# An MLP's first product over pairs of token blocks: seven block products for eight, and channel mix and MLP in two loops

## The chip, the cores and the metric

The kernel runs on one core of a Trainium2 chip. The metric is the device time of one execution in microseconds; the kernel before has a median of 2599.82 us over three runs (2597.92 to 2599.9).

## What is computed

Squared-relu attention over 4 sequences of 3072 tokens, an RWKV channel mix, and a squared-relu MLP, all in float32. Inputs are u, v (4 x 3072 x 256), z (4 x 3072 x 64), and weights.

```python
def _attn_ref(u, v, z):
    scale = 1.0 / S
    scores = scale * np.matmul(z, z.transpose(0, 2, 1))
    attn = np.maximum(scores, 0.0) ** 2
    return u * np.matmul(attn, v)

def _moe_ref(x, mu_k, mu_r, w_k, w_v, w_r):      # w_k 256 x 1024, w_v 1024 x 256, w_r 256 x 256
    xk = mu_k * x + (1.0 - mu_k) * x_prev        # x_prev: the token before
    xr = mu_r * x + (1.0 - mu_r) * x_prev
    k = np.maximum(xk @ w_k, 0.0)
    v = k * k @ w_v
    return 1.0 / (1.0 + np.exp(-(xr @ w_r))) * v

def _moe2_ref(x, w_in, w_out):                   # w_in 256 x 2048, w_out 2048 x 256
    r = np.maximum(x @ w_in, 0.0)
    return r * r @ w_out
```

## The kernel before

The work is done on transposed tiles: 128 features on partitions, a block of T = 512 tokens along the free dimension; there are NBLK = 24 blocks. Every float32 product is made of three matmuls on values split into a high and a low part (`split`, lines 80 to 85): high x high, low weight x high, high weight x low. One matmul is 128 x 128 weights against 128 x 512 values.

Attention comes first (`attention`, line 232): scores, squared relu, and the product with v, with the weights' conversion from float64 between. Its result goes to memory as `xT`, block by block. The first block of the channel mix (`up1`, `down1`) is already worked into its end.

Then `channel_mix_and_mlp` (line 499) runs over the 24 blocks, and within a block over 16 hidden tiles f of the MLP. At each f it makes the hidden tile f + 1 (`up2`: 6 matmuls at line 203, then relu and square on ScalarE, lines 157 and 158, cast and low part on VectorE, lines 84 and 85) and adds hidden tile f into the two output accumulators (`down2`: 6 matmuls, lines 534, 535 and 538). Between these, by the tables `before`, `after` and `aside` (lines 583 to 595), stand the pieces of the channel mix for the next block: `up1` and `down1` for its 8 hidden tiles, `gate_r`, `gate_v`, and `mix`. `gate_v` (line 515) multiplies the accumulators by the sigmoid and splits the product into the MLP's input, which stays on the chip. The schedule is manual: each engine runs its instructions in the order in which the program writes them.

The MLP's weights lie in memory as float32; `load_piece` and `split_piece` bring them in, the first two before the loop, the rest during block 0. A block's result is scaled out of the accumulators (line 560), transposed (line 561) and stored by four DMAs (`store`). For the last block the down products run in two halves of 256 tokens (`down2_half`, line 550), so that the first half's store overlaps the second's matmuls.

PSUM has eight banks: in this loop two for the channel mix's accumulators (`ps_v`), four for the MLP's (`ps_o`), two for hidden products (`ps_u`).

Of the kernel before, what the change touches and what calls it, by code (L numbers as in the profile page):

```python
# [7 lines left out]
F32 = mybir.dt.float32  # L8
# [8 lines left out]
Q = 32  # L17
# [4 lines left out]
def tile_relu2_attention__rwkv_channel_mix__relu2_mlp(  # L22
# [41 lines left out]
    perm = ctx.enter_context(tc.tile_pool(name="perm", bufs=1))  # L64
    raw_p = ctx.enter_context(tc.tile_pool(name="raw", bufs=3))
    ps_v = ctx.enter_context(tc.tile_pool(name="ps_v", bufs=1, space=PSUM))
    el = ctx.enter_context(tc.tile_pool(name="el", bufs=4))
# [6 lines left out]
    w_out32 = dram.tile([F2, D], F32, name="w_out32")  # L74
    xT = [dram.tile([D, S], F32, name=f"xT{b}") for b in range(B)]
# [136 lines left out]
    def down1(n, f):  # L212
        if f == 0:
            acc_v[n] = acc_tiles()
# [10 lines left out]
    AHEAD = 2  # L225

# [5 lines left out]
    def attention():  # L232
        with ExitStack() as st:
# [3 lines left out]
            ps_a = st.enter_context(tc.tile_pool(name="ps_a", bufs=1, space=PSUM))  # L237
            ps_w = st.enter_context(tc.tile_pool(name="ps_s", bufs=4, space=PSUM))
# [227 lines left out]
            for i in range(AHEAD):  # L466
                at_step(s + 12, load_piece, i)
# [31 lines left out]
    def channel_mix_and_mlp():  # L499
        with ExitStack() as st:  # L500
            wp = st.enter_context(tc.tile_pool(name="wp", bufs=1, reuse_waits="tile"))
            ps_o = st.enter_context(tc.tile_pool(name="ps_o", bufs=2, space=PSUM, reuse_waits="tile"))
            ps_w = st.enter_context(tc.tile_pool(name="ps_u", bufs=2, space=PSUM, reuse_waits="tile"))
            win = [wp.tile([P, 2, ND, T], F32R, name=f"win{i}") for i in range(F2 // T)]
            wout = [wp.tile([P, 2, G, D], F32R, name=f"wout{i}") for i in range(NF2 // G)]
            pools["ps"], pools["hidden"] = ps_w, (wp, "h", 6)
            gt, acc_o, x2, sig = {}, {}, {}, {}

            def gate_r(n, d):
                ps = up(lambda h, c, f: wr[:, h, c, f * P:(f + 1) * P], xr_t[n], d)  # L510
                t = wp.tile([P, T], F32, tag=f"sig{d}", name="sig")
                nc.scalar.activation(out=t, in_=ps, func=AF.Sigmoid)
                sig[n, d] = t

            def gate_v(n, d):
                if d == 0:
                    x2[n] = wp.tile([P, 2, ND, T], F32R, tag="x2", name="x2", bufs=2)
                t = el.tile([P, T], F32, tag="a", name="x2f")
                nc.vector.tensor_tensor(out=t, in0=acc_v[n][d], in1=sig.pop((n, d)), op=ALU.mult)
                split(x2[n][:, 0, d, :], x2[n][:, 1, d, :], t)  # L520

            def up2(n, f):
                q, r = divmod(f, T // P)
                ps = up(lambda h, c, f: win[q][:, h, c, r * P:(r + 1) * P], x2[n], f)
                gt[n, f] = relu2_split(ps, HS)

            def down2(n, f):
                if f == 0:
                    acc_o[n] = [ps_o.tile([P, T], F32, tag=f"o{d}", name=f"o{d}") for d in range(ND)]
                hi, lo = gt.pop((n, f))  # L530
                w, c = wout[f // G], f % G
                for d in range(ND):
                    ds_ = slice(d * P, (d + 1) * P)
                    nc.tensor.matmul(acc_o[n][d], lhsT=w[:, 0, c, ds_], rhs=hi, start=f == 0, stop=False)  # L534
                    nc.tensor.matmul(acc_o[n][d], lhsT=w[:, 1, c, ds_], rhs=hi, start=False, stop=False)  # L535
                for d in range(ND):
                    ds_ = slice(d * P, (d + 1) * P)
                    nc.tensor.matmul(acc_o[n][d], lhsT=w[:, 0, c, ds_], rhs=lo, start=False, stop=f == NF2 - 1)  # L538

            def down2_half(n, f, half):  # L540

                if f == 0:
                    acc_o[n, half] = ([ps_o.tile([P, T], F32, tag=f"o{d}", name=f"o{d}") for d in range(ND)] if half == 0
                                      else acc_tiles())
                (hi, lo), w, c = gt[n, f], wout[f // G], f % G
                ts = slice(half * T // 2, (half + 1) * T // 2)
                for d in range(ND):
                    ds_ = slice(d * P, (d + 1) * P)
                    for k, (h, x) in enumerate(((0, hi), (1, hi), (0, lo))):
                        nc.tensor.matmul(acc_o[n, half][d][:, 0:T // 2], lhsT=w[:, h, c, ds_], rhs=x[:, ts],  # L550
                                         start=f == 0 and k == 0, stop=f == NF2 - 1 and k == 2)

            def store(n, half=None, engines=(nc.sync,) * (P // Q)):

                y = raw_p.tile([P, T // Q, ND, Q], F32, tag="raw", name="y")
                a, size = acc_o.pop(n if half is None else (n, half)), T if half is None else T // 2
                m, t0 = size // Q, n * T + (half or 0) * size
                for d in range(ND):
                    t = wp.tile([P, T], F32, tag="yT", name="yT", bufs=2)
                    nc.scalar.mul(t[:, 0:size], a[d][:, 0:size], HS**-2)  # L560
                    nc.vector.transpose(y[:, 0:m, d, :], t[:, 0:size].rearrange("x (k q) -> x k q", q=Q))
                w = ND * Q
                for p, e in enumerate(engines):
                    e.dma_start(out=out[t0:t0 + size, p * w:(p + 1) * w].rearrange("(k q) f -> q k f", q=Q),
                                in_=y[p * Q:(p + 1) * Q, 0:m].rearrange("q k d r -> q k (d r)"))

            def split_piece(i):
                _, cs, fs = w_pieces[i]
                if i % 2 == 0:
                    t = win[fs.start // T]  # L570
                    split_raw(("w32", i), t[:, 0, cs], t[:, 1, cs])
                else:
                    t = wout[cs.start // G]

                    src = raws.pop(("w32", i)).rearrange("x c (p d r) -> x c p d r", d=ND, r=Q)
                    for d in range(ND):
                        split(*(t[:, h, :, d * P:(d + 1) * P].rearrange("x c (p r) -> x c p r", r=Q) for h in range(2)),
                              src[:, :, :, d], True)
                load_piece(i + AHEAD)

            before, after, aside = {}, {}, {}
            for f, unit, a in ((0, up1, 2), (1, down1, 1), (2, up1, 3), (3, down1, 2), (4, up1, 4), (5, down1, 3),
                               (6, up1, 5), (7, down1, 4), (8, up1, 6), (9, down1, 5), (10, gate_r, 0),
                               (11, gate_r, 1), (12, down1, 7)):
                before[f] = (1, unit, a)
            after[9] = (1, up1, 7)
            after[10] = (1, down1, 6)
            before[13], before[14] = (2, up1, 0), (2, up1, 1)  # L590
            before[15] = (2, down1, 0)
            aside[1], aside[2] = (1, mix, 1, 0), (1, mix, 1, 1)
            aside[3] = (2, load_x)
            aside[7], aside[9] = (2, mix, 0, 0), (2, mix, 0, 1)
            aside[12], aside[13] = (1, gate_v, 0), (1, gate_v, 1)
            assert NF1 == 8 and NF2 == 16

            def run(n, what):
                if what and n + what[0] < NBLK:
                    what[1](n + what[0], *what[2:])  # L600

            gate_r(0, 0)
            gate_v(0, 0)
            split_piece(0)
            gate_r(0, 1)
            gate_v(0, 1)
            split_piece(1)
            for f in range(3):
                up1(1, f)
            up2(0, 0)  # L610


            last, TAIL = NBLK - 1, 4
            for n in range(NBLK):
                for f in range(NF2):
                    if n < last:
# [5 lines left out]
                        if n == 0 and f % 4 < 2 and f // 4 < 3:  # L622
                            split_piece(2 + f // 4 * 2 + f % 4)
# [45 lines left out]
```

## Time and profile before

| | |
|---|---|
| runs | 2597.92, 2599.82, 2599.9 us; median 2599.82 |
| the profiled execution: its span, first to last instruction | 2597.3 us |
| what lies around that span | not recorded by itself; the three runs are 0.6 to 2.6 us above it |
| mean granted TensorE clock | 0.999 |
| from 0 to about 980 us | attention, with block 0 of the channel mix at its end |
| from about 980 to 2592 us | the channel mix of 23 blocks and the MLP of 24, interleaved |
| mean share of the DMA engines after 1000 us | 0.06 to 0.09 |

Matmuls are pipelined: a matmul's own duration overlaps that of the next, so the spacing of starts is the price of one. Idle time of an engine counts only where the engine that sets the end waits for it.

### The profile page before, as it was taken

How to read it: one execution, taken by the hardware profiler on the slowest of the kernel's cores; microseconds unless marked ns; L12 is line 12 of the kernel's file. 1: busy time of each engine (PE TensorE's matmuls, PEld its weight loads, DVE VectorE, ACT ScalarE, POOL GpSimd, SP SyncE). 2: the span in 40 equal slices, each digit the busy share in tenths (PEclk: the TensorE clock that was granted, in tenths of full speed). 3: DMA queues.
4: the chain of work that ended last, by engine and by line, in shares of the span. 5: the costliest groups of instructions: out<-in, count | busy, mean ns of one | idle time of the engine just before them, and what ended most of it. 6: DMA issues, size and time to landing. Idle time of an engine off the chain costs nothing.

```text
span 2597.3 us, 32434 instructions
## 1 busy us (share of the span) xinstructions
PE 2577.3 (99%) x11424; PEld 2132.5 (82%) x11424; DVE 1763.0 (68%) x3076; ACT 1511.8 (58%) x2529; POOL 0.2 (0%) x4
## 2 busy tenths in 40 slices
PE   7999999999999999999999999999999999999999
PEld 5887888888888888888888888888888888888888
DVE  8898989989898876555555555555555555555554
ACT  8766867777587555545545545555455445545544
POOL 0000000000000000000000000000000000000000
PEclk9999999999999999999999999999999999999999
DMA  7677777877867842000000000000000000000000
GB/s 196 168 208 182 209 200 181 223 204 188 230 192 201 211 128 65 17 17 17 17 17 17 17 17 17 17 10 16 17 17 11 14 17 17 17 17 17 17 9 17
DMA packets 301012, 218.68 MB, mean 84 GB/s; under 512 B 210480, under 2 KB 228912, under 8 KB 297776
## 3 DMA queue, kind: packets, MB, share of 16 engines
q1 hardware_dynamic: 299760, 216.34, 32.4%
q8 instruction: 89, 1.46, 0.2%
q14 instruction: 75, 0.61, 0.1%
q10 hardware_dynamic: 1088, 0.26, 0.1%
HBM read 124.28 MB, written 92.27 MB: 83 GB/s over the span
## 4 chain that ended last, share of the span: by engine, by line
PE 96%; DVE 1%; ACT 1%; DMA 1%; issue 0%; SPq 0%; DVEq 0%; ACTq 0%
PE ups L203 32%; PE v L375 9%; PE v L371 9%; PE v L372 9%; PE o L534 6%; PE o L538 6%; PE o L535 6%; PE v L222 3%; PE v L218 3%; PE v L219 3%; PE sps L344 3%; PE sps L343 3%; DMA mixed<-turned 0%; PE o L550 0%; PE v L550 0%
## 5 line engine op out<-in xcount | busy, mean ns | idle before, releaser
L157 ACT ACTIVATE a<-ups 128x512 f32<-128x512 f32 x576 | 344.3, 598 | 761.5 <-PE ups L203 745.4
L84 DVE CAST hhi<-a 128x512 fp32r<-128x512 f32 x568 | 241.9, 426 | 618.0 <-ACT a L158 586.1
L158 ACT ACTIVATE a<-a 128x512 f32<-128x512 f32 x912 | 576.8, 632 | 29.1
L203 PE MATMUL ups<-x,win 128*128 128x512 f32 x2304 | 584.2, 389 | 0.0
L203 PEld LDWEIGHTS ups<-x,win 128*128 128x128 f32 x2304 | 431.7, 188 | 89.2
L372 PE MATMUL v<-ahi,vhl 128*128 128x512 f32 x1152 | 448.8, 390 | 2.4 <-DVE vhl L278 2.4
L371 PE MATMUL v<-ahi,vhl 128*128 128x512 f32 x1152 | 448.8, 390 | 0.6 <-ACT ahi L338 0.6
L85 DVE TENSOR_TENSOR hlo<-a,hhi 128x512 fp32r<-128x512 f32 x568 | 393.5, 693 | 54.1 <-DVE hhi L84 2.3
L375 PE MATMUL v<-alo,vhl 128*128 128x512 f32 x1152 | 356.6, 391 | 4.2 <-DVE alo L353 4.1
L203 PE MATMUL ups<-mixed,wk 128*128 128x512 f32 x1152 | 292.0, 389 | 0.0
L534 PE MATMUL o<-hhi,wout 128*128 128x512 f32 x736 | 286.4, 389 | 0.7 <-DVE hhi L84 0.7
L535 PE MATMUL o<-hhi,wout 128*128 128x512 f32 x736 | 286.3, 389 | 0.0
L375 PEld LDWEIGHTS v<-alo,vhl 128*128 128x128 f32 x1152 | 215.4, 188 | 53.3 <-DVE alo L353 9.3
L372 PEld LDWEIGHTS v<-ahi,vhl 128*128 128x128 f32 x1152 | 216.6, 188 | 47.9 <-DVE vhl L278 2.8
L371 PEld LDWEIGHTS v<-ahi,vhl 128*128 128x128 f32 x1152 | 216.6, 188 | 46.3 <-ACT ahi L338 1.1
L203 PEld LDWEIGHTS ups<-mixed,wk 128*128 128x128 f32 x1152 | 216.2, 188 | 44.9
L157 ACT ACTIVATE a<-sps 128x512 f32<-128x512 f32 x336 | 199.3, 593 | 82.8 <-PE sps L344 75.1
L538 PE MATMUL o<-hlo,wout 128*128 128x512 f32 x736 | 226.6, 389 | 0.0
L353 DVE TENSOR_TENSOR alo<-a,ahi 128x512 fp32r<-128x512 f32 x336 | 220.9, 662 | 0.0
L314 DVE STREAM_TRANSPOSE turn<-a 128x512 f32<-128x512 f32 x240 | 207.8, 866 | 18.1 <-ACT a L158 16.7
L338 ACT CAST ahi<-mixed 128x512 fp32r<-128x512 f32 x220 | 129.2, 618 | 123.7 <-PE v L372 55.0
L339 DVE TENSOR_TENSOR alo<-mixed,ahi 128x512 fp32r<-128x512 f32 x220 | 146.7, 685 | 30.2 <-ACT ahi L338 27.5
(80 smaller groups left out, 2612.2 us busy)
## 6 DMA issues: line engine op xcount, KB each, us to landing
turned<-turn SPq DMA_DIRECT2D x60, 1024.0 KB, 5.1
mixed<-turned SPq DMA_DIRECT2D x220, 256.0 KB, 5.5
raw<-in_v_dram SPq DMA_DIRECT2D x24, 512.0 KB, 4.7
u<-in_u_dram SPq DMA_DIRECT2D x192, 64.0 KB, 4.4
xT<-uT SPq DMA_DIRECT2D x48, 256.0 KB, 2.2
out_dram<-y SPq DMA_DIRECT2D x92, 128.0 KB, 2.8
x<-xT SPq DMA_DIRECT2D x20, 513.0 KB, 3.8
zn<-in_z_dram SPq DMA_DIRECT2D x96, 64.0 KB, 3.8
```

Of the source, the lines that this page charges most:

```text
L84: nc.vector.tensor_copy(hi, src)
L85: nc.vector.tensor_tensor(out=lo, in0=src, in1=hi, op=ALU.subtract)
L157: nc.scalar.activation(out=a, in_=ps, func=AF.Relu, scale=scale)
L158: nc.scalar.activation(out=a, in_=a, func=AF.Square)
L203: nc.tensor.matmul(ps, lhsT=lhs(h, c, f), rhs=rhs[:, m, c, :], start=k == 0, stop=k == 3 * ND - 1)
L353: finish(lambda: nc.vector.tensor_tensor(out=lo, in0=a, in1=hi, op=ALU.subtract))
L371: nc.tensor.matmul(acc[n][d], lhsT=vt[:, 0, c, ds_], rhs=hi, start=first, stop=False)
L372: nc.tensor.matmul(acc[n][d], lhsT=vt[:, 1, c, ds_], rhs=hi, start=False, stop=False)
L375: nc.tensor.matmul(acc[n][d], lhsT=vt[:, 0, c, ds_], rhs=lo, start=False, stop=last)
L534: nc.tensor.matmul(acc_o[n][d], lhsT=w[:, 0, c, ds_], rhs=hi, start=f == 0, stop=False)
L535: nc.tensor.matmul(acc_o[n][d], lhsT=w[:, 1, c, ds_], rhs=hi, start=False, stop=False)
L538: nc.tensor.matmul(acc_o[n][d], lhsT=w[:, 0, c, ds_], rhs=lo, start=False, stop=f == NF2 - 1)
```

## The change

Channel mix and MLP become two loops. `channel_mix` runs the 23 remaining blocks alone, three hidden tiles ahead, and stores its gated result in memory (`x2d`, one buffer of 256 x 1024 for each pair of blocks). `mlp` then runs over 12 pairs of blocks and 8 groups each; a group is two hidden tiles of both blocks, that is a 2 x 2 by 2 x 2 block product of 128 x 128 weight blocks and 128 x 512 input blocks. It is formed with seven block products instead of eight, from sums of the weight blocks (S1 to S4, made once in `split_piece`) and of the input blocks (`prep_x2`, seven steps per pair, during the groups of the pair before). The four hidden blocks "11", "12", "21" and "22" come out of four PSUM banks by additions: u = P1 + bank 1, v = u + bank 2, "22" = v + bank 3, then, after the fifth to seventh products have been added into banks 0, 2 and 3, "11" = bank 0, "12" = u + bank 2, "21" = u + bank 3. Between the products stand the down products of the group before, in the order "22", "11", "12", "21". The last block has no halves any more, so the accumulators of a pair are scaled, transposed and stored whole. `ps_v`, `ps_a` (two banks each) and `ps_w` (four banks) now hold for the whole kernel, and `perm`, which has the channel mix's weights, is given back after the channel mix, for the second half of the MLP's weights.

The core of the diff (the removed function stands above; small moves of pools are left out):

```diff
+    x2d = [dram.tile([D, 2 * T], F32, name=f"x2d{p}") for p in range(NPAIR)]
...
+        def gate_v(n, d):
+            t = hp.tile([P, T], F32, tag="t", name="xo", bufs=6)
+            nc.vector.tensor_tensor(out=t, in0=acc_v[n][d], in1=sig.pop((n, d)), op=ALU.mult)
+            nc.sync.dma_start(out=x2d[n // 2][d * P:(d + 1) * P, n % 2 * T:(n % 2 + 1) * T], in_=t)
...
+        for i, (n, f) in enumerate(order):
+            if i + lead < len(order):
+                up1(*order[i + lead])
+            if f in (3, 5):
+                gate_r(n, (f - 3) // 2)
+            down1(n, f)
...
+        src = src.rearrange("x c (g i k) -> x c g i k", g=2, i=2)
+        a11, a12, a21, a22 = src[:, 0, :, 0], src[:, 1, :, 0], src[:, 0, :, 1], src[:, 1, :, 1]
+        sums = raw_p.tile([P, 2, 4, P], F32, tag="raw", name="sums")
+        s1, s2, s3, s4 = (sums[:, :, k] for k in range(4))
+        for out_, x, y, op in ((s1, a21, a22, ALU.add), (s2, s1, a11, ALU.subtract), (s3, a11, a21, ALU.subtract),
+                               (s4, a12, s2, ALU.subtract)):
+            nc.vector.tensor_tensor(out=out_, in0=x, in1=y, op=op)
+        hi, lo = win[q][:, 0], win[q][:, 1]
+        for k, x in ((A11, a11), (A12, a12), (A22, a22)):
+            split(hi[:, :, k], lo[:, :, k], x, True)
+        for g in range(2):
+            split(hi[:, g, S1:], lo[:, g, S1:], sums[:, g], True)
...
+        if k == 0:
+            x2_tmp[p] = t = hp.tile([P, 2, T], F32, tag="d13", name="d13")
+            nc.vector.tensor_tensor(out=t, in0=src[:, :, 1], in1=src[:, 0], op=ALU.subtract)
+        elif k == 3:
+            nc.vector.tensor_tensor(out=b12, in0=b22, in1=x2_tmp[p][:, 0], op=ALU.subtract)
...
+        def product(g, k):
+            p, i = g
+            q, r = divmod(i, 2)
+            b11, d24, d13, b2 = (ops[p, name] for name in ("b11", "d24", "d13", "b2"))
+            bank, w, x, first = ((0, A11, lambda h: b11[:, h], True), (1, S2, lambda h: d24[:, h, 0], True),
+                                 (2, S1, lambda h: d13[:, h, 0], True), (3, S3, lambda h: d13[:, h, 1], True),
+                                 (0, A12, lambda h: b2[:, h, 0], False), (2, S4, lambda h: b2[:, h, 1], False),
+                                 (3, A22, lambda h: d24[:, h, 1], False))[k]
+            if first:
+                banks[g, bank] = ps_w.tile([P, T], F32, tag="w", name="ups")
+            ps = banks[g, bank]
+            for m, (h, y) in enumerate(((0, 0), (1, 0), (0, 1))):
+                nc.tensor.matmul(ps, lhsT=win[q][:, h, r, w], rhs=x(y), start=first and m == 0, stop=m == 2,
+                                 skip_group_check=not first)
...
+        def add(g, to, bank, of):
+            tmp[g, to] = t = (brief if to == "v" else scratch)("s" + to)
+            nc.vector.tensor_tensor(out=t, in0=banks[g, bank], in1=tmp[g, of], op=ALU.add)
...
+        def side(g):
+            p, i = g
+            if i == 1 and p > 0:
+                store(p - 1, 1)
+                store(p - 1, 0)
+            if p + 1 < NPAIR:
+                if i == 0:
+                    load_x2(p + 1)
+                elif i >= 1:
+                    prep_x2(p + 1, i - 1)
+            if p == 0:
+                if i < 4:
+                    split_piece(4 + i)
+                if i + 2 < 4:
+                    load_piece(4 + i + 2)
...
+            def units():
+                for k in range(8):
+                    if g and k < 7:
+                        product(g, k)
+                        yield f"p{k}"
+                    if before:
+                        down2(before, k)
+                    yield f"d{k}"
+
+            for u in units():
+                if u == "p0":
+                    if before:
+                        relu(before, "21")
+                        square(before, "21")
+                        high(before, "12")
+                        low(before, "12")
+                    first_sum(g)
+                    if before:
+                        high(before, "21")
+                        low(before, "21")
+                elif u == "p1":
+                    add(g, "u", 1, "p1")
+                elif u == "p2":
+                    add(g, "v", 2, "u")
+                elif u == "p3":
+                    add(g, "22", 3, "v")
+                elif u == "d3" and g:
+                    side(g)
+                    relu(g, "22")
+                elif u == "p4":
+                    relu(g, "11")
+                    square(g, "22")
+                    square(g, "11")
+                    high(g, "22")
+                    high(g, "11")
+                elif u == "p5":
+                    add(g, "12", 2, "u")
+                    low(g, "22")
+                    relu(g, "12")
+                    square(g, "12")
+                elif u == "p6":
+                    add(g, "21", 3, "u")
...
+                    low(before, "21")
+                if before and before[1] == NF2 // 2 - 1:
+                    if u == "d5":
+                        evict(before[0], 1, 0)
+                        evict(before[0], 1, 1)
+                        if not g:
+                            store(before[0], 1, (nc.sync, nc.scalar) * 2)
```

**What stands in the queues.** Three places, for TensorE, VectorE and ScalarE.

TensorE in the middle of the MLP. Before, one step f of the loop (`ups` is a hidden product's bank, `o` the output accumulator, `v` the channel mix's, `hhi` and `hlo` the parts of a hidden tile):

```order
L534 MATMUL o0_17337<-hhi_17580,wout2_10042 128x512
L535 MATMUL o0_17337<-hhi_17580,wout2_10042 128x512
L534 MATMUL o1_17338<-hhi_17580,wout2_10042 128x512
L535 MATMUL o1_17338<-hhi_17580,wout2_10042 128x512
L538 MATMUL o0_17337<-hlo_17581,wout2_10042 128x512
L538 MATMUL o1_17338<-hlo_17581,wout2_10042 128x512
L203 MATMUL ups_17633<-mixed_17016,wk_75 128x512 x6
L203 MATMUL ups_17653<-x2_17193,win2_10038 128x512 x6
L203 MATMUL ups_17667<-mixed_17371,wr_77 128x512 x6
```

Now, the last steps of one group and the first of the next (`d13`, `b2`, `d24`, `b11` are prepared inputs, `v0` and `v1` output accumulators, `x3` three matmuls on one bank):

```order
L622 MATMUL ups_18301<-d24_17930,win1_10044 128x512 x3
L637 MATMUL v0_18111<-hhi_18276,wout1_10045 128x512
L638 MATMUL v0_18111<-hhi_18276,wout1_10045 128x512
L639 MATMUL v0_18111<-hlo_18277,wout1_10045 128x512
L637 MATMUL v1_18112<-hhi_18276,wout1_10045 128x512
L638 MATMUL v1_18112<-hhi_18276,wout1_10045 128x512
L639 MATMUL v1_18112<-hlo_18277,wout1_10045 128x512
L622 MATMUL ups_18353<-b11_17578,win2_15051 128x512 x3
L637 MATMUL v0_18091<-hhi_18321,wout1_10045 128x512
L638 MATMUL v0_18091<-hhi_18321,wout1_10045 128x512
L639 MATMUL v0_18091<-hlo_18322,wout1_10045 128x512
```

A hidden product had six matmuls on one bank in a row; now three matmuls of a product and three of a down step alternate, and no channel mix lies between.

VectorE where a finished block goes out. Before, at the end of a block (`a` is the squared hidden tile, `yT` the scaled output):

```order
L85 TENSOR_TENSOR hlo_11756<-a_11757,hhi_11755 128x512
L84 CAST hhi_11775<-a_11777 128x512
L85 TENSOR_TENSOR hlo_11776<-a_11777,hhi_11775 128x512
L561 STREAM_TRANSPOSE y_11796<-yT_11797 128x16x32
L561 STREAM_TRANSPOSE y_11796<-yT_11800 128x16x32
L84 CAST hhi_11814<-a_11816 128x512
L85 TENSOR_TENSOR hlo_11815<-a_11816,hhi_11814 128x512
L84 CAST hhi_11828<-a_11830 128x512
```

Now, in the first group of a pair, from "12" on (`s12`, `s21`, `s22`, `s11` are hidden blocks, `su` the sum u):

```order
L653 TENSOR_TENSOR s12_16577<-ups_16537,su_16532 128x512
L672 TENSOR_TENSOR hlo_16566<-s22_16550,hhi_16565 128x512
L681 STREAM_TRANSPOSE y_16585<-yT_16586 128x16x32
L681 STREAM_TRANSPOSE y_16585<-yT_16589 128x16x32
L653 TENSOR_TENSOR s21_16595<-ups_16546,su_16532 128x512
L672 TENSOR_TENSOR hlo_16569<-s11_16561,hhi_16568 128x512
L681 STREAM_TRANSPOSE y_16604<-yT_16605 128x16x32
L681 STREAM_TRANSPOSE y_16604<-yT_16608 128x16x32
L668 CAST hhi_16617<-s12_16577 128x512
L672 TENSOR_TENSOR hlo_16618<-s12_16577,hhi_16617 128x512
L668 CAST hhi_16623<-s21_16595 128x512
L672 TENSOR_TENSOR hlo_16624<-s21_16595,hhi_16623 128x512
```

Two transposes stood between hidden tiles; now four stand among the twelve steps from low "22" of one group to v of the next, and behind the last row shown come the sums u and v of the next group.

ScalarE at the start of the new MLP (`sig` is the channel mix's gate, `win2` a piece of the first weights, `raw` as it was loaded):

```order
L506 ACTIVATE sig_15018<-ups_15011 128x512
L649 COPY p1_15063<-ups_15059 128x512
L87 CAST win2_15051<-raw_15055 128x2x128 x3
L87 CAST win2_15051<-sums_15085 128x512 x2
L658 ACTIVATE s22_15081<-s22_15081 128x512
L658 ACTIVATE s11_15106<-ups_15059 128x512
L661 ACTIVATE s22_15081<-s22_15081 128x512
L661 ACTIVATE s11_15106<-s11_15106 128x512
L666 CAST hhi_15110<-s22_15081 128x512
L666 CAST hhi_15113<-s11_15106 128x512
```

and before, at the start of the interleaved loop:

```order
L512 ACTIVATE sig_10051<-ups_10044 128x512
L82 CAST win0_10036<-raw_9827 128x1024
L512 ACTIVATE sig_10069<-ups_10062 128x512
L82 CAST wout0_10040<-raw_9829 128x4x128 x2
L157 ACTIVATE a_10090<-ups_10081 128x512
L158 ACTIVATE a_10090<-a_10090 128x512
L157 ACTIVATE a_10104<-ups_10095 128x512
```

The weight piece's five casts, two of them on the sums that VectorE makes, now stand between the copy of the first product and the first relu; before, one cast of 1024 columns stood between two sigmoids.

## Rows read from the trace of the kernel before

**Rows 1.** the page's parts 1 and 4: engines' busy time, and shares of the last chain
```profile
PE 2577.3 (99%) x11424; PEld 2132.5 (82%) x11424; DVE 1763.0 (68%) x3076; ACT 1511.8 (58%) x2529; POOL 0.2 (0%) x4
...
PE 96%; DVE 1%; ACT 1%; DMA 1%; issue 0%; SPq 0%; DVEq 0%; ACTq 0%
```
**Rows 2.** stretches: us, then busy PE, PEld, DVE, ACT, POOL (count), PEclk, DMA, GB/s
```profile
993.00:2540.00 1547.00, 1547.00 (x6826) 1280.96 (x6826) 875.03 (x1548) 777.72 (x1278) 0.00 (x0) 1.00 0.08 17
```
**Rows 3.** groups by line, forms apart: the MLP's products (line, engine, tiles, count, busy, mean)
```profile
L203 PE MATMUL ups<-x,win 128*128 128x512 f32 x2304 | 584.2, 389 | 0.0
...
L534 PE MATMUL o<-hhi,wout 128*128 128x512 f32 x736 | 286.4, 389 | 0.7 <-DVE hhi L84 0.7
```
**Rows 4.** order of time at the end (start us, us, engine, line, operation)
```profile
2585.34 0.40 PE L550 MATMUL o<-hhi,wout 128*128 128x256 f32 x2
...
2592.41 0.28 PE L550 MATMUL v<-hlo,wout 128*128 128x256 f32 x1
2592.43 0.74 ACT L560 ACTIVATE yT<-v 128x256 f32<-128x256 f32 x2 [2.20 <-PE v L550]
...
2593.68 0.88 ACTq L564 DMA_DIRECT2D out_dram<-y  x2
```
**Rows 5.** groups by line: ScalarE and VectorE
```profile
L158 ACT ACTIVATE a<-a 128x512 f32<-128x512 f32 x912 | 576.8, 632 | 29.1
...
L85 DVE TENSOR_TENSOR hlo<-a,hhi 128x512 fp32r<-128x512 f32 x568 | 393.5, 693 | 54.1 <-DVE hhi L84 2.3
...
L157 ACT ACTIVATE a<-ups 128x512 f32<-128x512 f32 x576 | 344.3, 598 | 761.5 <-PE ups L203 745.4
...
L84 DVE CAST hhi<-a 128x512 fp32r<-128x512 f32 x568 | 241.9, 426 | 618.0 <-ACT a L158 586.1 <-PE v L550 14.6
...
L188 DVE SCALAR_TENSOR_TENSOR xm<-x,mu,m 128x512 f32<-128x512 f32 x96 | 71.4, 744 | 1.0 <-ACT m L186 1.0
...
L519 DVE TENSOR_TENSOR x2f<-v,sig 128x512 f32<-128x512 f32 x48 | 32.8, 684 | 0.9 <-ACT sig L512 0.9
...
L561 DVE STREAM_TRANSPOSE y<-yT 128x512 f32<-128x512 f32 x46 | 30.0, 690 | 13.3 <-ACT yT L560 13.3
...
L560 ACT ACTIVATE yT<-o 128x512 f32<-128x512 f32 x46 | 25.0, 596 | 27.1 <-PE o L538 27.1
...
L85 DVE TENSOR_TENSOR win<-raw,win 128x1024 fp32r<-128x1024 f32 x4 | 4.9, 1218 | 0.0
L82 ACT CAST wout<-raw 128x512 fp32r<-128x512 f32 x8 | 4.5, 614 | 0.0
L82 ACT CAST win<-raw 128x1024 fp32r<-128x1024 f32 x4 | 4.1, 1036 | 0.0
```
**Rows 6.** order of time near 1400 us
```profile
1396.93 1.09 ACT L560 ACTIVATE yT<-o 128x512 f32<-128x512 f32 x2 [1.23 <-PE o L538]
...
1397.57 1.30 DVE L561 STREAM_TRANSPOSE y<-yT 128x512 f32<-128x512 f32 x2 [0.60 <-ACT yT L560]
...
1401.04 1.52 PE L203 MATMUL ups<-x,win 128*128 128x512 f32 x6
...
1402.60 0.60 ACT L157 ACTIVATE a<-ups 128x512 f32<-128x512 f32 x1 [1.46 <-PE ups L203]
```
**Rows 7.** DMA issues by line: count, KB each, median us to landing
```profile
out_dram<-y SPq DMA_DIRECT2D x92, 128.0 KB, 2.8
...
raw<-w_in SPq DMA_DIRECT2D x4, 512.0 KB, 4.6
```
**Rows 8.** order of time of TensorE at 991 us
```profile
991.55 0.50 PE L534 MATMUL o<-hhi,wout 128*128 128x512 f32 x1 [0.73 <-DVE hhi L84]
```
**Rows 9.** near the start: a wait of TensorE, and the stretch behind it
```profile
14.50 0.50 PE L372 MATMUL v<-ahi,vhl 128*128 128x512 f32 x1 [2.36 <-DVE vhl L278]
...
14.40:18.60 4.20, 4.10 (x11) 3.03 (x12) 3.30 (x7) 4.11 (x9) 0.00 (x0) 0.59 0.55 77
```
**Rows 10.** groups by line: the transpose of turn
```profile
L314 DVE STREAM_TRANSPOSE turn<-a 128x512 f32<-128x512 f32 x240 | 207.8, 866 | 18.1 <-ACT a L158 16.7 <-DMA turned<-turn 0.5
```

More of the change, by code (lines that the diff above doesn't have):

```diff
@@ L497, in attention @@
             assert not todo, todo.keys()
[L499 to L531, printed above, removed]
-                for d in range(ND):
[L533 to L616, printed above, removed]
-                        up2(*divmod(n * NF2 + f + 1, NF2))
-                        run(n, before.get(f) if n or f else (1, down1, 0))
-                        down2(n, f)
-                        run(n, after.get(f))
-                        run(n, aside.get(f))
-                        if n == 0 and f % 4 < 2 and f // 4 < 3:
-                            split_piece(2 + f // 4 * 2 + f % 4)
-                    elif f < NF2 - TAIL:
-                        for k in range(1 if f == 0 else f + 2, f + 5 if f == NF2 - TAIL - 1 else f + 3):
-                            up2(n, k)
-                        for half in range(2):
-                            down2_half(n, f, half)
-                        gt.pop((n, f))
-                if n < last:
-                    store(n)
-            for half in range(2):
-                for f in range(NF2 - TAIL, NF2):
-                    down2_half(last, f, half)
-                store(last, half, (nc.sync, nc.scalar) * 2)
@@ new lines, in tile_relu2_attention__rwkv_channel_mix__relu2_mlp, with w_tiles, split_piece @@
+    x2_raw, x2_tmp, ops, win, wout = {}, {}, {}, {}, {}
+    N_PREP = 7
+    A11, A12, A22, S1, S2, S3, S4 = range(7)
+    def w_tiles(pool, q):
+        win[q] = pool.tile([P, 2, 2, 7, P], F32R, name=f"win{q}")
+        wout[q] = pool.tile([P, 2, G, D], F32R, name=f"wout{q}")
+    def split_piece(i):
+        q = i // 2
+        src = raws.pop(("w32", i))
+        if i % 2:
+            src = src.rearrange("x c (p d r) -> x c p d r", d=ND, r=Q)
+            for d in range(ND):
+                split(*(wout[q][:, h, :, d * P:(d + 1) * P].rearrange("x c (p r) -> x c p r", r=Q) for h in range(2)),
+                      src[:, :, :, d], True)
+            return
+        src = src.rearrange("x c (g i k) -> x c g i k", g=2, i=2)
[10 more added lines that the diff above has]
+            split(hi[:, g, S1:], lo[:, g, S1:], sums[:, g], True)
@@ L637, in tile_relu2_attention__rwkv_channel_mix__relu2_mlp @@
     with tc.manual_schedule():
         attention()
-        channel_mix_and_mlp()
+        hp = ctx.enter_context(tc.tile_pool(name="hp", bufs=1, reuse_waits="tile"))
+        w3 = ctx.enter_context(tc.tile_pool(name="w3", bufs=1, reuse_waits="tile"))
+        pools["ops", 0] = ctx.enter_context(tc.tile_pool(name="ops0", bufs=1, reuse_waits="tile"))
+        for q in range(2):
+            w_tiles(w3, q)
+        channel_mix()
+        held.close()
+        w4 = ctx.enter_context(tc.tile_pool(name="w4", bufs=1, side="right", reuse_waits="tile"))
@@ L642 @@
+        pools["ops", 1] = ctx.enter_context(tc.tile_pool(name="ops1", bufs=1, side="right", reuse_waits="tile"))
+        for q in range(2, 4):
+            w_tiles(w4, q)
+        for i in range(2):
+            load_piece(4 + i)
+        mlp()
 _INS = ["u", "v", "z", "moe_mu_k", "moe_mu_r", "moe_w_k", "moe_w_v", "moe_w_r", "moe2_w_in", "moe2_w_out"]
```

133 lines of the change are left out of this document (126 added, 7 removed).

## The prediction

> **What bounds the kernel now.** I read the page's busy shares first, then the chain of waits, the stretches, the groups by line, and last the order of time at three places. TensorE is busy 99% of the span and holds 96% of the chain that ended last [rows 1]: time is bought only with fewer or quicker matmuls, and lost only where TensorE has to wait. From 993 to 2540 us, channel mix and MLP interleaved, it is busy for all of 1547.00 us over 6826 matmuls, 0.2266 us each, while VectorE works 875 and ScalarE 778 us [rows 2]. A matmul's own 389 ns in the groups [rows 3] overlap the next one's; 0.2266 us is the price that counts, and every full matmul here has the same shape.
>
> **Matmuls removed.** The program has 2304 matmuls for the MLP's first product and 3 x 736 for full-width down products [rows 3]. The last block's down products are 192 half-width ones: 60 of them start between 2585.34 and 2592.41 [rows 4], 59 steps, 0.120 us each. After: 12 pairs x 8 groups x 7 products x 3 = 2016, and 96 x 24 = 2304 full-width down matmuls. Full ones fall from 2304 + 2208 to 2016 + 2304, by 192: 192 x 0.2266 = 43.5 us. The half ones go: 192 x 0.120 = 23.0 us. **Together -66.5 us**, all on the path.
>
> **Work that moves to the vector engines.** An MLP group is 45 matmuls, 10.20 us. In it VectorE does five adds out of PSUM (684 ns, as x2f), two casts (426) and four differences (693): 7.04 us. A pair adds seven preparation steps, four of 1024 columns (1218) and three of 512 (about 690), 6.9 us, and four transposes (690), 2.8 us: 8.26 us per group on average [rows 5]. ScalarE does one copy and one relu out of PSUM, seven relus or squares in place (632), two casts (614): 6.85 us, with preparation and eviction 7.6. Both fit in 10.20 us.
>
> Whether they are in time is a matter of the order. Count from the start of a group's first product; product or down step number k (from 0, alternating) ends at 0.68 x (k + 1), and its result is seen 0.20 us later: a chain of six starting at 1401.04 has its last slot over at 1402.40, and ScalarE starts at 1402.60 [rows 6]. In an ordinary group the fourth product is seen at 4.96, "22" is summed at 5.64, its relu ends at 6.3, relu "11" at 6.9, two squares at 8.2, cast "22" at 8.8, its low part at 9.5; the next group's first down step wants that low part for its third matmul at 11.3. Slack 1.8 us. The sixth product of the next group, over bank 2, wants the sum v there at 17.0 and would have it some 3 us earlier. So **an ordinary group costs nothing**, under cover of 1.8 us.
>
> **The first group of a pair (11 times).** There four evictions and transposes of the pair before stand in both queues. ScalarE: relu "11" can start at 6.32 and is followed by two squares, two casts, relu and square of "12", and only then the first eviction: 0.598 + 4 x 0.632 + 2 x 0.614 + 0.596 = 4.95, so 11.27. The next group's first down step writes that accumulator at 10.88 and waits 0.4. VectorE, from 11.3: two transposes, s21, low "11", two transposes, cast and low "12", cast and low "21", u, v: 4 x 0.690 + 3 x 0.684 + 3 x 0.693 + 2 x 0.426 = 7.74 us; v is done at 19.1, wanted at 17.0. Wait 2.1 us in all. But two independent evictions take 1.09 us, not 1.19, and two transposes 1.30, not 1.38 [rows 6]: back to back, 0.08 to 0.10 us of each is hidden. With some five ScalarE and nine VectorE steps shortened so, v is done at about 18.0: wait 1.0 us. Bounds 1.0 and 2.2; these queues are full there, so I take a value near the lower one, 1.3: **11 x 1.3 = +14.3 us** (11 to 24).
>
> **The start of the MLP.** Nothing is interleaved with the first group, 7 x 0.68 = 4.76 us of products. Its side work splits a weight piece, and this stands ahead of relu "22" and "11" on ScalarE and after s22 on VectorE. The piece's load is issued behind the last two stores of the channel mix, which wait for VectorE's two gates (0.20 + 2 x 0.684 = 1.6 us); with the stores' issue, 2.1 us; landing takes 4.6 us [rows 7]: 6.7. Then four sums of 256 columns, which have no row: between half of 0.684 (0.34) and the whole; a line through 512 and 1024 columns gives 0.42, so 1.7 us; two casts of 0.614; two relus: 10.8. The next group's first product needs bank 0 from relu "11" and was due at 4.76: 6.1 us. Then its first down step waits for squares and cast, 1.0, and for the low part, 0.3. A second such piece in the third group takes VectorE to 7.04 + 1.2 + 4.3 = 12.6 us against 10.2: about 1.8 after slack. **Together +9.2 us**, 5 if the load is early, 13 if the short steps cost as much as long ones.
>
> While TensorE stands for 6 us its clock may fall. Early in the trace, after a wait of 2.4 us for VectorE, a stretch of 4.2 us was granted 0.59 of the clock [rows 9], that is, partly the 1.2 GHz level; lost there: 4.2 x 0.41 = 1.7 us. I count it once: **+1.7**; between 0 and 3.
>
> **The channel mix alone.** A block is 108 matmuls, 24.5 us; VectorE does 8 x 1.12 + 4 x (0.744 + 0.426 + 0.693) + 2 x 0.684 = 17.8 us [rows 5]. Hidden products are made three steps ahead: 8.2 us from the end of one to its down step, of which relu, square, cast and low need 2.5. The worst extra load, a weight piece (4.3 us of VectorE), fits into the rest. Cost 0, at most 2. If that cover went, down1 would wait for hlo. At its start the wait of 0.73 us for hhi [rows 8], behind four weight splits, goes with these: **-0.7**; next late is nothing, down1 begins 8.2 us after attention and needs its parts at 6.7.
>
> **Memory round trip and queues.** 48 stores and 12 loads pass through SP. A store waits for one gate; behind it wait the x load (wanted two steps later) and nothing else. The load of the next pair goes out a whole group, 10 us, before its first use, and 512 KB land in 4.6 us [rows 7]; even twice that is hidden. Cost 0.
>
> **The end.** Before: last matmul at 2592.41, last stores issued from 2593.68, end 2597.3 [rows 4]: 4.9 us. After, full-width: eviction, transpose (0.6 + 0.7 instead of 0.4 + 0.4) and 128 KB per store (2.8 us to land [rows 7]): **+1.2**.
>
> **Sum.** 2597.3 - 66.5 + 14.3 + 9.2 + 1.7 - 0.7 + 1.2 = 2556.5 us of span. The three runs lie 0.6 to 2.6 above the profiled span, their median 2.5; so I forecast **2559 us**. About 0.2%, 5 us, is what a measurement here tells from no change.
>
> **Rivals.**
> (a) *The clock falls at every pair.* Each of the 11 waits is followed by a slow stretch of 1.7 us [rows 9]: 2559 + 19 = 2578. For it: the trace has one such stretch after a wait of that size. Against: that one was just after the kernel's start. The Trainium skill, "TensorE: Matmul & The Clock Gate", section "HAM oscillation — how this bites in real kernels", says that repeated waits of the array between bursts send the clock back to half each time, so that every burst begins slow; by that rule applied to all 11 waits this rival would hold. The trace bears it out at one place only. Chance 0.12.
> (b) *Slower: VectorE becomes the bound of every MLP group.* Place: VectorE's 8.26 us of steps in the 10.20 us of a group. It decides from 10.9 us on, where 0.7 x 96 = 67 us is given back; that is 32% more per step. Price: at 11.1 us, 96 x 0.9 = 86 us instead of the 14.3, 2559 + 72 = 2631. For it: the transpose of turn takes 866 ns, that of y 690, 25% for the same size [rows 10, 5], so a step's price can depend on its addresses, and the new operands are strided. Against: the adds and differences have the form of rows that stand at 684 to 693 beside a busy TensorE. Chance 0.05.
> (c) *The boundaries are absorbed*, because steps pack tighter still: 2559 - 14.3 = 2545. Chance 0.10.
> (d) *The change removes less than it says*, because a product of three matmuls that accumulates on a bank just read is delayed at every group by 0.5 us: 96 x 0.5 = 48, so 2607 less the boundary's 14, 2593, near no change. The order has these waits, and the read ended 3 us before. Chance 0.03.
> My forecast has the remaining 0.70.
>
> **How the numbers follow.** Sum of the low bounds: 11 + 5 + 0 for 14.3 + 9.2 + 1.7 gives 2550; of the high ones, 24 + 13 + 3 + 2, 2576. The range 2546 to 2579 takes in most of (c) and (a), and leaves out (b) and (d). Faster 0.92 (forecast, (a), (c)); same 0.03 ((d)); slower 0.05 ((b)).
>
> **What would show it.** TensorE: 11040 matmuls, still 0.2266 us apart. In the MLP the waits of TensorE should be few: L622 for VectorE's v (L653) once per pair, 1 to 2 us, L637 for evictions under 0.5; a gap of about 6 us on L622 for relu L658 near 1545 us; PEclk below full there at most. L511 and L585 appear in no wait of TensorE. Waits of L622 or L639 in every group would prove me wrong towards (b) or (d); PEclk below 1 at every 82 us towards (a).

## The result, and the profile after

The changed kernel takes 2557.2 us (median of four runs, 2556.26 to 2561.02) against 2599.82: ratio 0.984, 95% interval 0.9826 to 0.9854. The profiled span is 2554.5 us, 42.8 below that of before; 2559 us and a span of 2556.5 were forecast. The profiled execution is the fastest of the four.

The page's parts 1 and 4 of the kernel after, to be read beside [rows 1]:

```profile
PE 2516.1 (98%) x11040; PEld 2074.1 (81%) x11040; DVE 2008.3 (79%) x3382; ACT 1668.8 (65%) x2879; POOL 0.2 (0%) x4
...
PE 91%; DVE 4%; ACT 3%; issue 1%; DMA 0%; SPq 0%; DVEq 0%; ACTq 0%
```

There are 11040 matmuls, as counted. TensorE's share of the chain falls from 96 to 91%: VectorE and ScalarE now hold pieces of the path. Stretches of the kernel after, columns as in [rows 2]:

```profile
980.00:1543.00 563.00, 563.00 (x2486) 466.28 (x2485) 407.11 (x717) 319.47 (x524) 0.00 (x0) 1.00 0.15 49
1543.00:1580.00 37.00, 29.97 (x122) 23.84 (x120) 27.90 (x50) 21.11 (x41) 0.00 (x0) 0.91 0.30 100
...
1725.00:2549.00 824.00, 813.46 (x3575) 669.86 (x3573) 614.39 (x982) 532.16 (x949) 0.00 (x0) 1.00 0.11 24
```

The channel mix alone leaves no gap, at 563.00 / 2486 = 0.2265 us per matmul, the spacing of before. The start of the MLP has gaps and a clock below full; in the long stretch after it TensorE is not quite filled. Who TensorE waited for in the kernel after (us in total, times, longest):

```profile
PE ups L622 <- DVE sv L653: 8.4, 11, 0.8
...
PE v L637 <- ACT hhi L666: 7.3, 2, 6.3
```

That is all there is behind attention: eleven waits for the sum v, one at each start of a pair, and two at the MLP's start.

| term | forecast, us | measured, us |
|---|---|---|
| attention, unchanged code | 0 | -1.0 (its end moves between 978.6 and 981.3 over the runs below) |
| matmuls | -66.5 | -66.5 (11040, same spacing) |
| eleven starts of a pair | +14.3 | +11.9 |
| start of the MLP, clock with it | +10.9 | +10.6 |
| start of the channel mix | -0.7 | -1.5 |
| the end | +1.2 | +3.8 |
| sum | -40.8 | -42.7 |

The measured terms come so: from the first gate product (978.75) to the end of the last matmul's slot (2545.94) are 1567.2 us, of which 6816 matmuls at 0.22663 take 1544.7; 22.5 us of waits are left, in the same count before 1.5. Each start of a pair costs 1.05 to 1.10, 1.08 on average (the first of them below), the MLP's start has the rest: about 6.4 in its second group, 1.5 in its third, and 2.2 in matmuls at the slower clock between them. Of the 1.5 before, 1.0 lies at the wait of [rows 8]; the rest is spread over the loop. From the last slot to the end are 8.6 us, before 4.8.

The first start of a pair in order of time, kernel after (the first row is the group's first product):

```profile
1630.97 0.84 PE L622 MATMUL ups<-b,win 128*128 128x512 f32 x3
...
1641.06 2.04 ACT L680 ACTIVATE yT<-v 128x512 f32<-128x512 f32 x4
...
1641.67 1.30 DVE L681 STREAM_TRANSPOSE y<-yT 128x512 f32<-128x512 f32 x2 [1.50 <-ACT yT L680]
...
1644.07 1.29 DVE L681 STREAM_TRANSPOSE y<-yT 128x512 f32<-128x512 f32 x2
...
1647.37 0.68 DVE L653 TENSOR_TENSOR su<-ups,p 128x512 f32<-128x512 f32 x1
...
1647.75 0.39 PE L639 MATMUL v<-hlo,wout 128*128 128x512 f32 x1
1648.16 0.69 DVE L653 TENSOR_TENSOR sv<-ups,su 128x512 f32<-128x512 f32 x1
1648.91 0.96 PE L622 MATMUL ups<-b,win 128*128 128x512 f32 x3 [0.77 <-DVE sv L653]
```

VectorE works from 1641.67 to 1648.85 with hardly a pause: 7.18 us for twelve steps. Before them it stood 1.50 us, until ScalarE had the first eviction ready; so ScalarE's queue starts this one. The product was due at 1647.98 and starts at 1648.91, as soon as v is there: 0.93 us, and a little more behind it. From step to like step:

```profile
1641.17 0.84 PE L622 MATMUL ups<-b,win 128*128 128x512 f32 x3
...
1652.44 0.84 PE L622 MATMUL ups<-b,win 128*128 128x512 f32 x3
```

These are the starts of one product in two groups that follow each other, 11.27 us apart where 45 matmuls take 10.20: 1.07 us.

The start of the MLP, kernel after:

```profile
1549.29 0.84 PE L622 MATMUL ups<-b,win 128*128 128x512 f32 x3
1551.09 1.02 ACT L87 CAST win<-raw 128x256 fp32r<-128x256 f32 x3 [5.10 <-DMA raw<-w_in]
1551.09 0.42 DVE L576 TENSOR_TENSOR sums<-raw 128x256 f32<-128x256 f32 x1 [2.69 <-DMA raw<-w_in]
...
1554.25 0.57 ACT L658 ACTIVATE s<-ups 128x512 f32<-128x512 f32 x1
...
1556.42 0.79 PE L637 MATMUL v<-hhi,wout 128*128 128x512 f32 x1 [6.29 <-ACT hhi L666]
```

The chain is the forecast one: landing, sums, casts, two relus, squares, cast. One step differs: the next group's first product (1549.29) did not wait for relu "11" (1554.25).

### The profile page after: what moved, and what is told of

Read it like the earlier page. It is cut to its first block, busy times and chain, and to the rows that moved or that the text cites. A ratio compares the mean times of both kernels' runs of the same rounds, so it can differ in the third digit from the quotient of the medians.

```text
span 2554.5 us, 31628 instructions
## 1 busy us (share of the span) xinstructions
PE 2516.1 (98%) x11040; PEld 2074.1 (81%) x11040; DVE 2008.3 (79%) x3382; ACT 1668.8 (65%) x2879; POOL 0.2 (0%) x4
## 4 chain that ended last, share of the span: by engine, by line
PE 91%; DVE 4%; ACT 3%; issue 1%; DMA 0%; SPq 0%; DVEq 0%; ACTq 0%
PE ups L622 15%; PE ups L208 13%; PE v L376 10%; PE v L373 10%; PE v L372 10%; PE v L637 6%; PE v L639 6%; PE v L638 6%; PE v L224 3%; PE v L227 3%; PE v L223 3%; PE sps L345 3%; PE sps L344 3%; DVE y L681 1%; ACT s L658 1%; ACT s L661 1%
## 5 line engine op out<-in xcount | busy, mean ns | idle before, releaser
L658 ACT ACTIVATE s<-s 128x512 f32<-128x512 f32 x288 | 180.7, 627 | 331.7 <-DVE s L653 331.7
L163 ACT ACTIVATE a<-a 128x512 f32<-128x512 f32 x528 | 334.0, 632 | 16.8
L622 PE MATMUL ups<-d,win 128*128 128x512 f32 x1152 | 324.3, 390 | 0.0
L637 PE MATMUL v<-hhi,wout 128*128 128x512 f32 x768 | 299.9, 390 | 7.3 <-ACT hhi L666 7.3
L639 PE MATMUL v<-hlo,wout 128*128 128x512 f32 x768 | 299.6, 390 | 0.0
L638 PE MATMUL v<-hhi,wout 128*128 128x512 f32 x768 | 299.5, 390 | 0.0
L672 DVE TENSOR_TENSOR hlo<-s,hhi 128x512 fp32r<-128x512 f32 x384 | 264.7, 689 | 35.3 <-ACT hhi L666 19.8
L162 ACT ACTIVATE a<-ups 128x512 f32<-128x512 f32 x192 | 114.8, 598 | 237.8 <-PE ups L208 209.8
L622 PEld LDWEIGHTS ups<-d,win 128*128 128x128 f32 x1152 | 217.0, 188 | 45.3
L622 PE MATMUL ups<-b,win 128*128 128x512 f32 x864 | 243.9, 391 | 8.4 <-DVE sv L653 8.4
L661 ACT ACTIVATE s<-s 128x512 f32<-128x512 f32 x384 | 231.2, 628 | 6.1
```

What stands on the lines that cost most here:

```text
L162: nc.scalar.activation(out=a, in_=ps, func=AF.Relu, scale=scale)
L163: nc.scalar.activation(out=a, in_=a, func=AF.Square)
L622: nc.tensor.matmul(ps, lhsT=win[q][:, h, r, w], rhs=x(y), start=first and m == 0, stop=m == 2, skip_group_check=not first)
L637: nc.tensor.matmul(acc[p, b][d], lhsT=w[:, 0, c, ds_], rhs=hi, start=first, stop=False)
L638: nc.tensor.matmul(acc[p, b][d], lhsT=w[:, 1, c, ds_], rhs=hi, start=False, stop=False)
L639: nc.tensor.matmul(acc[p, b][d], lhsT=w[:, 0, c, ds_], rhs=lo, start=False, stop=last)
```

## Experiments

e2, e3a, e4, e5 and e7 were executed once each. Executions of one kernel lie up to 4.8 us apart, so where such a run moves the span by less, it is the waits in its trace that decide.

**e1: two of the four transposes a group later.**

```diff
+            if b == 0 and p + 1 < NPAIR:
+                put_off.append(turn_out)
+            else:
+                turn_out()
...
             if i == 1 and p > 0:
                 store(p - 1, 1)
+            if i == 2 and p > 0:
                 store(p - 1, 0)
...
                 elif u == "p6":
                     add(g, "21", 3, "u")
                     low(g, "11")
+                    if g[1] == 1:
+                        while put_off:
+                            put_off.pop(0)()
```

> Two of the four transposes of a finished pair (those of its first block) move from the end of the first group of the next pair to the end of the second; nothing else moves. Queue theory (the wait of 0.93 us at each of 11 pair starts is the backlog of VectorE's twelve steps ahead of the sum v): the backlog loses two transposes, 1.30 us, which is more than the wait, so the 11 waits of L622 for L653 go; span 2554.5 - 11 x 1.04 = 2543 us. Rival (the wait comes from ScalarE, whose four evictions push back the copy of the first product and so u and v): ScalarE's order is unchanged, so the 11 waits stay at about 0.77 us as the profile counts them, span about 2554.

Measured: 2545.0 us (2544.49 to 2545.89), ratio to the kernel before 0.9792 (0.9776 to 0.9809); span 2543.1. TensorE's waits in e1:

```profile
PE sps L344 <- DVE zz L268: 7.5, 1, 7.5
PE v L637 <- ACT hhi L666: 7.2, 2, 6.2
```

The stores of these transposes move a group later too, which the expectation did not say; TensorE waits for no store. The wait for v is gone from the list, all eleven times, and the span is 11.4 us shorter, though attention ended at 980.04, 1.3 later. Of the 12.7 us behind attention 11.9 are the eleven starts, and 0.8 a shorter stretch at the slower clock at the MLP's start. ScalarE's order was unchanged, so the rival, that its four evictions alone make the wait by a late copy, fails. They still start VectorE's queue; a run that moves the evictions was not made.

**e2: two transposes twice.**

```diff
-            nc.vector.transpose(y_t[p, b][:, :, d, :], t.rearrange("x (k q) -> x k q", q=Q))
+            for _ in range(1 + b):
+                nc.vector.transpose(y_t[p, b][:, :, d, :], t.rearrange("x (k q) -> x k q", q=Q))
```

> The two transposes of a finished pair's second block are made twice, 2 x 12 more VectorE steps and nothing else. Queue theory: each of the 11 waits grows by two transposes, 1.30 us, 11 x 1.30 = 14.3; with 1.4 at the end of the kernel, span 2554.5 + 15.7 = 2570 us, waits of L622 for L653 about 2.1 us each. Rival (ScalarE sets the wait): VectorE has slack there, waits unchanged, span about 2556.

Measured: span 2572.5 us, +18.0, 1.4 of it at the end. VectorE at the first start of a pair, and TensorE's waits, in e2:

```profile
1641.99 2.80 DVE L682 STREAM_TRANSPOSE y<-yT 128x512 f32<-128x512 f32 x4 [1.51 <-ACT yT L680]
```

```profile
PE ups L622 <- DVE sv L653: 16.1, 11, 1.5
...
PE v L639 <- DVE hlo L672: 5.5, 11, 0.5
```

Four transposes take 2.80 us where two took 1.30. The wait for v grows by 0.7 each time, and a second one of 0.5 appears for the low part of "11", earlier in the same queue. By the spacing of TensorE's starts the eleven places cost 16.2 us more, some 3 of which the list does not count as waiting; attention ended 0.4 later. That is 1.5 us for each place, as much as the two transposes add to VectorE's queue: the backlog is VectorE's.

**e3: the weight pieces two groups later.**

```diff
-                if i < 4:
-                    split_piece(4 + i)
-                if i + 2 < 4:
-                    load_piece(4 + i + 2)
+                if 2 <= i < 6:
+                    split_piece(2 + i)
+                if 2 <= i < 4:
+                    load_piece(4 + i)
```

> The four weight pieces that the MLP still splits in groups 0 to 3 of the first pair are split in groups 2 to 5 (they are used from group 4 on). Theory (the wait of 6.3 us in the second group is the load's landing and five casts that stand ahead of the first relus on ScalarE): the wait shrinks to the time from relu to cast, about 1.2 us, the clock stays at 1.00, so 5.1 + about 2.3 us for the slow stretch are saved; a wait of about 1 us stays behind each of the two pieces of the first weights. Span 2554.5 - 7.4 + 1.0 = 2548 us. Rival (the empty first group, with nothing to do beside its seven products, is itself what TensorE waits for): the wait stays above 4 us, span 2552 or more.

Measured: 2551.16 us (2549.98 to 2553.9), ratio 0.9817 (0.9802 to 0.9831); span 2549.3, though attention ended 1.1 us later than in the kernel after: 6.3 us saved, 7.4 - 1.0 expected. A wait of TensorE and a stretch of e3:

```profile
PE v L637 <- ACT hhi L666: 2.5, 3, 1.0
```

```profile
1550.00:1555.00 5.00, 4.00 (x17) 2.66 (x16) 3.33 (x6) 4.94 (x11) 0.00 (x0) 1.00 0.97 347
```

The wait of 6.3 is 1.0 now, and the clock stays full. Behind the empty first group 1.0 us of waiting is left, 1.6 with the slower starts after it.

**e3a: only the loads early.** `load_piece(4)` and `(5)` move into the channel mix's last block.

> Only the loads of the first two of these pieces go out earlier, some 14 us before the channel mix ends; the splits stay. Theory: the 2.7 us that VectorE waited for the landing go, casts and relus then follow; the wait in the second group falls from 6.3 to about 3.6 us; whether the clock still falls after a wait of that length is open: with the fall span 2552, without it 2549.5 us. Rival (the casts are what counts, the load is hidden behind the copy and the sums): unchanged, 2554 us.

Measured: span 2551.7 us, as expected with the slow stretch. The wait and the stretch behind it in e3a:

```profile
1554.04 0.51 PE L639 MATMUL v<-hhi,wout 128*128 128x512 f32 x1 [3.50 <-ACT hhi L668]
```

```profile
1553.80:1557.00 3.20, 2.96 (x8) 2.10 (x9) 2.95 (x6) 3.14 (x7) 0.00 (x0) 0.72 0.64 204
```

Landing was 2.8 of the 6.3 us; of the other 3.5, 1.0 stays in e3 too, and 2.5 go with the sums and casts ahead of the relus.

**e4, e6, e8: the end.** e4 issues the last pair's first stores by SP alone:

```diff
-                            store(before[0], 1, (nc.sync, nc.scalar) * 2)
+                            store(before[0], 1)
```

> The four stores of the last pair's second block are all issued by SP instead of two by ScalarE; nothing else. Theory (the end is 8.6 us long because ScalarE issues two stores, 0.93 us that wait for VectorE's transposes, ahead of the last two evictions): the last evictions start at the end of the down products instead of 1.4 us after, the last transposes end about 1.6 us earlier, and the time from the last matmul to the end falls from 8.8 to about 7.5 us, as SP's queue is now the longer one. Rival (the end is set by the landing of 128 KB stores and their issue on SP): 8.8 us stays.

Measured: span 2555.1 us; from the last matmul's start to the end 8.4 us, 8.7 in the kernel after. e4's end:

```profile
2545.66 2.75 DVE L681 STREAM_TRANSPOSE y<-yT 128x512 f32<-128x512 f32 x4 [1.87 <-ACT yT L680]
...
2546.65 0.39 PE L639 MATMUL v<-hlo,wout 128*128 128x512 f32 x1
2547.08 4.97 SPq L686 DMA_DIRECT2D out_dram<-y  x6
2548.45 0.99 ACTq L686 DMA_DIRECT2D out_dram<-y  x2
```

The last transposes of the kernel after, whose last matmul starts at 2545.71:

```profile
2547.76 1.30 DVE L681 STREAM_TRANSPOSE y<-yT 128x512 f32<-128x512 f32 x2 [1.64 <-ACT yT L680]
```

The transposes did end earlier, 1.8 us after the last matmul's start and not 3.3, and it bought 0.3 us: my theory on the end fell. e6 has e1, e3 and e4 together:

> Two transposes later, weight pieces later and the last stores on SP, together. If the three waits are apart from each other: 2554.5 - 11.4 - 6.3 - 1.3 = 2535.5 us of span, median of runs about 2537.5. If the moved pieces and the moved transposes meet in VectorE's queue (they do not share a group: pieces in the first pair, transposes from the second on) less is saved.

Measured: 2538.96 us (2537.97 to 2539.08, five runs), ratio to the kernel before 0.9767 (0.9754 to 0.9781); span 2536.7. The savings add up but for the end: of the 22.5 us of waits 4.4 are left. This beats both kernels. e8 is e6 with all eight last stores behind the evictions, shared by SP and ScalarE:

> As e6_all, but the last eight stores are written behind all four last evictions and shared again by SP and ScalarE, four each. Theory after e4 (once ScalarE's stores no longer stand ahead of its evictions, the end is set by the issue of six stores on SP, 4.97 us, and the landing of the last): SP issues four, in some 3.8 us, ScalarE four in about 2 us after its last eviction; the time from the last matmul's start to the end falls from 8.4 to about 7 us, span 2536.7 - 1.4 = 2535 us. Rival (the landing of eight stores at once sets the end, whoever issues them): 8.4 us stays, 2537 us.

Measured: 2539.39 us (2538.18 to 2540.62), span 2537.6; 8.6 us at the end. Issues and stretches of e8 (the last two columns: DMA share, GB/s):

```profile
2529.43 3.73 SPq L693 DMA_DIRECT2D out_dram<-y  x4
2529.47 3.79 ACTq L693 DMA_DIRECT2D out_dram<-y  x4
```

```profile
2530.00:2532.00 2.00, 0.00 (x0) 0.00 (x0) 0.76 (x2) 0.01 (x1) 0.00 (x0) 0.94 0.83 123
2532.00:2534.00 2.00, 0.00 (x0) 0.00 (x0) 0.00 (x0) 0.00 (x0) 0.00 (x0) 0.50 1.03 190
2534.00:2536.00 2.00, 0.00 (x0) 0.00 (x0) 0.00 (x0) 0.00 (x0) 0.00 (x0) 0.50 0.99 203
```

Whoever issues them, the eight stores (1 MB) fill all 16 DMA engines for about 6 us. That these set the end fits three orders of issue (the kernel after, e4 and e6, e8) with nearly the same 8.4 to 8.7 us; a kernel with fewer bytes at the end was not tried.

**e5: an eighth product.**

```diff
-            for m, (h, y) in enumerate(((0, 0), (1, 0), (0, 1))):
+            for m, (h, y) in enumerate(((0, 0), (1, 0), (0, 1)) * (1 + (k == 6))):
```

> The seventh product of every group is made twice, into the same bank (block 22 of the weights counted double, so the hidden blocks 21 and their results are not the MLP's): 3 x 96 = 288 more matmuls, as many as a block product of eight would have, and no other instruction. Theory (matmuls are the bound; everything else of the change only adds waits): + 288 x 0.2266 = 65.3 us, less what the longer groups give back at the 11 waits, 0.68 each, 7.5: span 2554.5 + 57.8 = 2612 us, so the two loops without the scheme's saved product would be about 15 us slower than the kernel before. Rival (the MLP is paced by VectorE and ScalarE, and matmuls have slack): less than + 30 us, 2585 or below.

Measured: span 2612.1 us, +57.6. The page's part 1 of e5:

```profile
PE 2582.9 (99%) x11328; PEld 2129.4 (82%) x11328; DVE 2016.2 (77%) x3382; ACT 1686.4 (65%) x2879; POOL 0.2 (0%) x4
```

The first of the eleven starts in e5:

```profile
1653.76 0.39 PE L639 MATMUL v<-hlo,wout 128*128 128x512 f32 x1
1654.25 0.96 PE L622 MATMUL ups<-b,win 128*128 128x512 f32 x3
```

The eleven waits are not in its list; by the spacing of starts 0.39 us of each 1.08 is left. So the loss is 65.3 us of matmuls less 7.6 at the eleven starts. The gain is the matmuls' alone: these two loops with eight block products instead of seven are 15 us slower than the kernel before.

**e7: more work for VectorE.**

```diff
+                    for _ in range(2):
+                        spare = brief("spare")
+                        nc.vector.tensor_tensor(out=spare, in0=tmp[g, "u"], in1=tmp[g, "u"], op=ALU.add)
                     add(g, "12", 2, "u")
```

> Two additions of 512 columns without use are added to VectorE's queue in every group, ahead of the sum for block 12: 192 instructions, some 125 us of VectorE's time. Theory (an ordinary group has slack, VectorE waits there for ScalarE and TensorE): hidden in ordinary groups; in the first two groups of a pair up to about 1 us more, so span between 2555 and 2566 us. Rival (b) of the prediction (VectorE is near the bound of every group): 0.6 us or more for each of 96 groups, 2612 us or above.

Measured: span 2557.1 us, +2.6, of which 2.5 lie in attention, which ended at 981.27. From the groups and the waits of e7:

```profile
L746 DVE TENSOR_TENSOR spare<-su 128x512 f32<-128x512 f32 x192 | 123.6, 685 | 0.0
```

```profile
PE ups L622 <- DVE sv L653: 8.5, 11, 0.8
```

124 us of VectorE's time vanish in its waits of an ordinary group. Placed ahead of block 12, they do not even lengthen the eleven waits: there VectorE still stands 1.5 us for ScalarE's first eviction behind them.

## Why the prediction was right

The large term, 66.5 us of matmuls, held to a tenth, and the waits that are left lie where they were forecast, at the starts. Among the small terms there was luck: the others fell 4.5 us short of their forecasts (the eleven starts 2.4, attention, whose code is unchanged, 1.0, the channel mix's start 0.8, the MLP's 0.3), and the end came out 2.6 above its own, which leaves the span only 2 us below the forecast.

- *Matmuls removed.* -66.5 us, exact. e5 puts 288 matmuls back and loses 57.6 us: 65.3 less what the eleven waits shrink by.
- *An ordinary group costs nothing.* TensorE's list has no wait in a group other than those at the starts, and e7 bears the slack out. Rival (b) is refuted: the adds take 685 to 692 ns, the rows' price.
- *The first group of a pair.* The mechanism was right (e1, e2). The mis-sized term: I took 1.3 us, it is 1.08, near the lower bound. The twelve steps take 7.18 us back to back, not 7.74, and ScalarE has the first eviction ready 10.7 us after the group's first product (1630.97), not 11.27: the shortening that [rows 6] shows for two steps of a kind holds along both queues. So v is done 17.9 us after that product; the working had 18.0 against 17.0 wanted, and the step from its wait of 1.0 to 1.3 was the error. The 0.4 us given to TensorE's wait for the evictions did not come. Rival (c) failed, as the starts are not absorbed, and rival (d) has no wait in the list.
- *The start of the MLP.* 10.9 us forecast, 10.6 measured. One step failed: "The next group's first product needs bank 0 from relu 11". It starts 5 us before that relu, so it cannot have been in that bank (which one it got, the trace does not show), and the whole wait falls on its down step. That hangs on the same queue of ScalarE, but the product is now done under the wait: 6.4 us in the second group where 7.4 were forecast, and 1.5 in the third for 1.8. The sum came near because the clock cost more than forecast. The steps of 256 columns, bounded between 0.34 and 0.68, take 0.42.
- *The clock.* A fall was expected once, at 1.7 us. It came there and cost about 2.2 us, by the spacing of starts; and rival (a) failed: the eleven waits of 0.8 us leave PEclk at 1.00 from 1725 to 2549. Behind the wait of 6.3 us, kernel after:

```profile
1556.40:1560.00 3.60, 3.58 (x9) 2.77 (x9) 3.53 (x7) 3.54 (x7) 0.00 (x0) 0.50 0.49 166
```

Nine matmuls took the time of sixteen, at the 1.2 GHz level. The Trainium skill, "TensorE: Matmul & The Clock Gate", section "HAM oscillation — how this bites in real kernels", has each burst of matmuls start cold after a wait for a transfer that is longer than the burst itself. That the clock is low behind a long wait agrees with the trace here, for the waits of 6.3 and 3.5 us. The eleven waits, 0.8 us in some 82 us of matmuls, are not the section's case, and rival (a) took its rule too far.
- *The end.* "+1.2" was the step that failed; it is +3.8. I priced one store's landing, 2.8 us, where eight stores of a whole pair go out together. How long the DMA engines are full at the end, in the kernel before and (three lines) after:

```profile
2594.50:2596.00 1.50, 0.00 (x0) 0.00 (x0) 0.00 (x0) 0.00 (x0) 0.00 (x0) 0.82 0.98 172
```

```profile
2547.00:2553.00 6.00, 0.00 (x0) 0.00 (x0) 1.30 (x2) 1.08 (x2) 0.00 (x0) 0.82 1.00 171
2548.00:2550.00 2.00, 0.00 (x0) 0.00 (x0) 1.06 (x2) 0.21 (x1) 0.00 (x0) 1.00 0.99 170
2550.00:2552.00 2.00, 0.00 (x0) 0.00 (x0) 0.00 (x0) 0.00 (x0) 0.00 (x0) 0.71 1.00 171
```

The halves of the kernel before had half a block to store after the last matmul (four stores of 64 KB, 1.5 us); now it is a pair of blocks (eight of 128 KB, 6.0 us). The difference of 4.5 us, which partly runs beside the last evictions, has the size of the 3.8; that it is their cause is argued from this and from e4, e6 and e8, not tested by itself.

## What to carry to other kernels

When TensorE is the bound, count its instructions first: here the saving came in full, and the rest of the forecast is a search for the places where the new queues are late. These are the seams (the first group, the change from one result to the next, the end), not the steady groups; there, add up the in-order queue from the event that starts it to the value that TensorE needs. A step that feeds the bound engine belongs ahead of one that merely must be done some time: moving two transposes and four weight pieces, with no work saved, bought 18.1 (e6) of the 22.5 us of waits.

## What was not expected of the hardware

Eight stores of 128 KB, issued within 5 us, keep all 16 DMA engines busy for 6 us at about 170 GB/s, and the end came 8.4 to 8.7 us after the last matmul's start for three orders of issue. TensorE's clock was granted at half after a wait of 6.3 us, and fell after one of 3.5 us, but not after waits of 1.0 us or of 0.8 us repeated every 83 us.
